# Linear attention and gated unit on one core: K's maxima and exponentials bank by bank, Q's maxima as rows, another opening and a new list

## The chip, the cores and the metric

One Trainium2 chip, one of its cores, one launch. The time is the device's microseconds for one execution. The kernel before took 234.67 us as the median of three runs (234.15 to 235.96). A profiled execution is a run by itself and has its own time, given below.

## The reference, cut to what matters

```python
def phi(x):                                        # x: 8 batches, 8 heads, 576 tokens, 64
    proj = np.einsum('bhsd,df->bhsf', x, w_phi)    # 128 features
    proj = proj - np.max(np.abs(proj), axis=-1, keepdims=True)
    return np.concatenate([np.exp(proj), np.exp(-proj)], axis=-1)
q_p, k_p = (phi(q), phi(k))
kv = np.einsum('bhsf,bhsd->bhfd', k_p, v);  z = np.sum(k_p, axis=2)
num = np.einsum('bhsf,bhfd->bhsd', q_p, kv)
den = np.einsum('bhsf,bhf->bhs', q_p, z)[..., None] + 1e-06
x = num / den                                      # heads side by side: 8 x 576 x 512
# gate_pre: a causal convolution of 5 taps along the tokens, per channel, of x
return (sigmoid(gate_pre) * (x @ w_val)) @ w_out
```

Note that the second half is exp(-proj) of the shifted projection: for the token t with maximum m it is exp(-p + m), so the shift has to reach both signs.

## The kernel before, in words

**Units.** A batch has 8 heads, taken as 4 pairs; a pair is a unit (numbers 0 to 31), with 512 of its 576 tokens. The 64 tokens left over in each of a batch's heads make one more unit (32 to 39, the tail units). After four units and a tail unit the batch's attention is complete, and its gated unit can run.

**A unit's steps**, with the names that the list uses: T transposes the unit's K and Q on the tensor engine (PE) into one bank of PSUM; C copies them out as bf16 (DVE or ACT). PK projects K (two banks, 4 x 2 x 128 columns of float32), MK takes the maxima of its absolute values over the features (DVE, line 441, one instruction over both banks), K0 and K1 take exp(p) and exp(-p) (ACT, line 475, one instruction each over both banks). E takes the exponentials of K's maxima (ACT, line 459) and V multiplies V's rows with them (POOL, line 505), so that K's shift is put into V. PA projects Q a first time with tokens on the partitions, only so that MQ (DVE, line 441) can take its maxima; PQ projects Q again with features on the partitions (line 541), SA subtracts the maxima in PSUM by 8 matmuls of a broadcast weight against a negative identity (line 564), and X0 and X1 take the two exponentials (ACT, line 466). KV (line 518) sums up K's features against V, KM copies the sum out, N (line 610) multiplies Q's features with it, XN divides (DVE, lines 628 and 630), and XP transposes the result by DMA or, late in the program, on PE (line 655). Per batch there are GF (the five taps as 80 matmuls, line 689), TH (tanh on ACT, line 705), VA and VB (x times w_val, line 710), GV (gate times value on DVE, line 726), OA and OB (times w_out, line 739), OE (ACT or DVE, lines 748 and 750) and the stores ST and SL; GT, VT, HT, GW, OT, OF and SU are the same for the 64 tokens left over (lines 779 to 824).

**What sets the order.** A string ORDER is a hand-made list of tokens. A token `PK.3@4,5:W` says: step PK of unit 3, PSUM banks 4 and 5, variant W; `:D`, `:A`, `:P` name DVE, ACT or POOL. Each engine works off its instructions in the order of the list, and semaphores hold them until their inputs are there. All eight banks of PSUM are dealt out by hand. Two engines that read the same bank are kept apart: a K exponential and the maxima of the same banks run one after the other. What stands ahead of the list (loads of the first unit, constants) was put in order by the scheduler. FL is a filler, a matmul of zeros.

**The opening.** The first unit's K comes in two halves on the queues of SP and ACT (line 169), Q follows in one piece on SP's queue (line 163), w_phi twice on ACT's queue (line 183) and is cast by `W.0:A` into W2 (line 223). All of w_val (1 MB) is loaded at the start (line 317) and cast by POOL in eleven pieces (CV). The other loads (LD) go through POOL's queue, with a cast. w_out is loaded by eleven DMAs on SP's queue (line 324) and cast whole on POOL (`CO.0:P`, the row `WOUT`).

## Time and profile before

| | |
|---|---|
| median of three runs | 234.67 us |
| the profiled execution | 232.76 us |
| its span (first to last instruction) | 231.0 us |
| PE busy | 206.4 us, 3758 matmuls |
| ACT busy | 185.8 us, 288 instructions |
| DVE busy | 178.7 us, 281 instructions |
| POOL busy | 134.2 us, 187 instructions |
| granted clock of PE | 1.00 in every stretch |

The span leaves out 1.8 us that lie around the program. An engine's busy time is the union of its instructions; where they follow one another without a wait, the next one starts before the one ahead has ended, so that a row's mean duration times its count is more than its busy time. A matmul's end is modelled. The views used are the table of busy time by stretches (`windows`), the groups of instructions by line and shape, the waits, the timeline, and the chain of waits, which is followed back from the last instruction.

### The profile page before, as it was taken

The page shows a single profiled execution, that of the slowest core. Times are in us where ns is not written, and L with a number is a line of the kernel's source. Part 1 is how long each engine was busy: PE and PEld are TensorE (multiplying, and loading weights), DVE is VectorE, ACT ScalarE, POOL GpSimd, SP SyncE. Part 2 cuts the span into 40 slices and gives each one's busy share as a digit, 9 for nine tenths or more (in the row PEclk, how much of TensorE's full clock was granted, in tenths as well). Part 3 has the DMA queues.
Part 4 walks back from the last instruction along what each step waited for, and adds up shares of the span by engine and source line. Part 5 has one row for each costly group of instructions (what it writes and reads, how often), then busy time and mean ns, then how long its engine had stood idle before and what let it go on. Part 6 is the DMA issues. An engine that isn't in the chain of part 4 may idle for free. (4 is left out here: it accounts for less than half of the span.)

```text
span 231.0 us, 8642 instructions
## 1 busy us (share of the span) xinstructions
PE 206.4 (89%) x3758; PEld 142.7 (62%) x3784; DVE 178.7 (77%) x281; ACT 185.8 (80%) x288; POOL 134.2 (58%) x187
## 2 busy tenths in 40 slices
PE   1567889899989589999998999899999999999996
PEld 0244677677658356568666866686668756675542
DVE  7298699989977669788886999699988897356341
ACT  2299999999879668988898989799898999652450
POOL 8479999995798199673316909720439248600000
DMA  6999999399999959999995198281682066103646
GB/s 130 263 186 161 173 145 144 37 194 199 129 179 220 217 63 160 146 187 136 128 181 192 27 139 164 70 116 26 154 168 71 4 93 184 45 7 91 176 144 184
DMA packets 41424, 31.36 MB, mean 136 GB/s; under 512 B 16933, under 2 KB 37413, under 8 KB 41386
## 3 DMA queue, kind: packets, MB, share of 16 engines
q0 software_dynamic: 20816, 14.90, 45.3%
q1 hardware_dynamic: 19946, 15.16, 32.6%
q10 hardware_dynamic: 624, 0.75, 1.1%
q8 instruction: 29, 0.48, 0.9%
q14 instruction: 9, 0.07, 0.1%
HBM read 32.58 MB, written 9.44 MB: 182 GB/s over the span
## 5 line engine op out<-in xcount | busy, mean ns | idle before, releaser
L505 POOL TENSOR_TENSOR VT<-vN,EA 128x1024 bf16<-128x1024 bf16 x32 | 61.1, 1910 | 22.7 <-issue 8.8
L475 ACT ACTIVATE KT<-PS 128x1024 bf16<-128x1024 f32 x64 | 63.9, 1041 | 5.1 <-PE PS L406 3.9
L466 ACT ACTIVATE QT<-PS 128x1024 bf16<-128x1024 f32 x64 | 62.1, 1043 | 6.0 <-PE PS L564 5.8
L441 DVE TENSOR_REDUCE MKA<-PS 128x8 f32<-128x1024 f32 (+1 forms) x40 | 44.3, 1112 | 5.5 <-PE PS L399 2.2
L441 DVE TENSOR_REDUCE MQA<-PS 128x8 bf16<-128x1024 f32 (+1 forms) x40 | 44.5, 1113 | 3.3 <-PE PS L406 2.1
L710 PE MATMUL PS<-XT,WVAL 128*128 128x512 bf16 x128 | 35.3, 380 | 0.2
L739 PE MATMUL PS<-WOUT,GV 128*128 128x512 bf16 x110 | 31.2, 380 | 2.5 <-POOL WOUT L225 1.8
L726 DVE SCALAR_TENSOR_TENSOR GV<-GATE,PS 128x512 bf16<-128x512 bf16 x32 | 21.3, 683 | 10.9 <-ACT GATE L705 6.1
L496 POOL TENSOR_TENSOR VTZ<-vN,EA 64x512 bf16<-64x512 bf16 x16 | 16.7, 1044 | 19.6 <-ACT EA L459 17.6
L564 PE MATMUL PS<-nident,MQA 128*128 128x128 bf16 x288 | 23.0, 220 | 2.8 <-issue 2.1
L225 DVE COPY T<-PS 128x1024 bf16<-128x1024 bf16 x29 | 19.6, 685 | 7.0 <-PE PS L366 6.7
L630 DVE TENSOR_TENSOR XN<-PS,RCPA 128x512 bf16<-128x512 f32 x32 | 22.1, 692 | 1.2 <-DVE RCPA L628 0.2
L564 PEld LDWEIGHTS <-MQA 128*128 128x128 bf16 x288 | 17.4, 98 | 8.4 <-issue 3.6
L518 PE MATMUL PS<-VT,KT 128*128 128x65 bf16 x512 | 21.9, 194 | 0.8 <-POOL VT L509 0.3
L610 PEld LDWEIGHTS <-QT 128*128 128x128 bf16 x512 | 19.3, 97 | 5.1 <-issue 0.5
L518 PEld LDWEIGHTS <-KT 128*128 128x128 bf16 x512 | 19.1, 98 | 4.4 <-issue 1.1
L610 PE MATMUL PS<-KVSA,QT 128*128 128x65 bf16 x512 | 21.0, 193 | 0.4 <-issue 0.2
L748 ACT ACTIVATE OS<-PS 128x512 f32<-128x512 f32 x24 | 13.8, 599 | 8.5 <-PE PS L739 6.3
L705 ACT ACTIVATE GATE<-PS 128x1024 bf16<-128x1024 f32 x16 | 16.0, 1039 | 5.2 <-PE PS L689 5.2
L406 PE MATMUL PS<-W,T 64*128 64x128 bf16 x392 | 18.7, 221 | 1.1 <-DVE MQA L441 0.4
L406 PEld LDWEIGHTS <-T 64*128 64x128 bf16 x392 | 13.0, 95 | 9.4 <-issue 5.7
L366 PE MATMUL PS<-ident_bf,kN 128*128 128x128 bf16 x128 | 12.8, 224 | 4.1 <-DVE kN L225 3.5
(93 smaller groups left out, 328.4 us busy)
## 6 DMA issues: line engine op xcount, KB each, us to landing
out_dram<-OS SPq DMA_DIRECT2D x28, 256.0 KB, 3.7
kN<-in_k_dram POOLq DMA_DIRECT2D x14, 320.0 KB, 7.4
vN<-in_v_dram POOLq DMA_DIRECT2D x14, 320.0 KB, 7.5
qN<-in_q_dram POOLq DMA_DIRECT2D x7, 576.0 KB, 9.0
OS<-in_moe_w_val_dram SPq DMA_DIRECT2D x1, 1024.0 KB, 10.4
out_dram<-OSt SPq DMA_DIRECT2D x8, 128.0 KB, 2.4
vN<-in_v_dram POOLq DMA_DIRECT2D x4, 160.0 KB, 7.4
OS<-in_moe_w_out_dram SPq DMA_DIRECT2D x8, 64.0 KB, 6.8
```

Of the source, the lines that this page charges most:

```text
L406: nc.tensor.matmul(PS[:, bank[par], c0 + blk * P:c0 + (blk + 1) * P], u.T[r, i, blk, :], W2[r, :], start=True, stop=True,)
L441: read(nc.vector.tensor_reduce(tokdst(dst[:, 0:n, :], wide, u.tail), tokview(bank, x, u, wide), AX.X, ALU.max, apply_absolute_value=True,) ...
L466: read(nc.scalar.activation(dst, banks(*bank)[:, :, 0:n * P].rearrange("p r (x t) -> p r x t", t=dst.shape[-1]), AF.Exp, scale=1.0 if ft = ...
L475: read(nc.scalar.activation(tokdst(u.KT[:, ft, :, :, :], u.PKwide, u.tail), tokview(u.PK, 0, u, u.PKwide), AF.Exp, scale=1.0 if ft == 0 el ...
L505: e.tensor_tensor(u.VT[:, :, :, 0:D], x.unsqueeze(1).to_broadcast([P, 2, n, D]), w.unsqueeze(3).to_broadcast([P, 2, n, D]), ALU.mult,)
L518: nc.tensor.matmul(PS[:, bank[0], c:c + E1], u.KT[:, ft, j // 2, j % 2, :], u.VT[:, ft, j, :], start=(ft == 0 and j == 0), stop=False, ski ...
L564: nc.tensor.matmul(PS[:, u.PQ[par], blk * P:(blk + 1) * P], MQA[:, i, blk, par:par + 1].to_broadcast([P, P]), nident[:, :], start=False, s ...
L610: nc.tensor.matmul(PS[:, bank[c // 2], x * E1:(x + 1) * E1], u.QT[:, ft, c, h2, :, :].rearrange("p j t -> p (j t)"), kv[:, ft, h2, :], sta ...
L630: read(nc.vector.tensor_tensor(u.XN[:, :, :, :], nv[:, :, :, 0:D], rc.unsqueeze(3).to_broadcast([P, 2, 4, D]), ALU.mult,), u.N)
L710: nc.tensor.matmul(PS[:, m.val[jt], :], WVAL[:, dt, jt * P:(jt + 1) * P], planes(xt(m.b), slice(0, P), dt, 4), start=(dt == 0), stop=(dt = ...
L726: read(nc.vector.scalar_tensor_tensor(out=m.GV[:, jt, :, :, :].rearrange("p n i t -> p (n i t)"), in0=m.GATE[jt // 2][:, jt % 2, :], scala ...
L739: nc.tensor.matmul(PS[:, bank, :], lhs(jt), WOUT[:, jt, :], start=(jt == 0), stop=(jt == 3))
```

## The change

**K bank by bank.** MK is replaced by MA and MB, one maximum per bank (line 503), and K0 and K1 by KA and KB, which take both exponentials of one bank (line 532). A bank is so released when its own pieces are done. Tail units keep the old steps.

**Q's maxima as rows.** For units 2 to 31 MQ writes its maxima into a row block MQX; a new step MT transposes it on PE (line 554, one matmul and one bank), MC copies it out as MQT (14 on ACT, 16 on DVE, 128x128), and SA's 8 matmuls take a broadcast column of the negative identity as weight and 64 of MQT's rows as input (line 661), where they took 128 rows.

**Opening.** Q's first load is in two halves, on the queues of SP and ACT behind K's. w_phi is one DMA on POOL's queue that reads it twice and casts it (line 195), so W is gone. T.0 is cut in two (T.0 for K, TX.0 for Q), and so is C.0 (C.0 on DVE, CX.0 on ACT). The constants of DVE stand in program order and all ahead of the first cast of Q. w_val's load stands later in the list (LW.0, after E.2).

**Early casts.** CV is four pieces, CO four pieces on DVE and POOL, and DIAGF's 16 copies are four (DF). w_out comes in six DMAs, and stands in the list before the first batch's gated unit, where it stood behind the second batch's gate steps (GT.1).

**List.** All tokens are dealt again over engines and banks: three V move from POOL to DVE, six OE from ACT to DVE, four T from DVE to ACT; 11 of 15 wide projections of K (PK:W, four matmuls of 256 columns) become narrow (eight of 128 with 64 rows).

On DVE at the start of the program (the instructions in order; XT, DIAGF, VTZ and MQX are constants, GV holds the loaded float32, T is the transposed unit) stood before:

```order
L213 MEMSET DIAGF 128x1280
L225 CAST kN<-GV 128x640
L198 CAST ident_123<-ident_bf 5x5
L255 TENSOR_SCALAR nident<-ident_bf 128x128
L225 CAST qN<-GV 128x576
L225 COPY T<-PS 128x1024 x2
L441 TENSOR_REDUCE MQA<-PS 128x2x4
L441 TENSOR_REDUCE MKA<-PS 128x2x4
```

and now:

```order
L224 MEMSET DIAGF 128x1280
L226 MEMSET VTZ_138 128x1040
L230 MEMSET MQX 128x256
L268 MEMSET VTZ_139 128x1040
L241 CAST qN<-GV 128x576
L241 COPY T<-PS 128x512
L503 TENSOR_REDUCE MKA<-PS 128x4 x2
L241 COPY T<-PS 128x1024
L472 TENSOR_REDUCE MQA<-PS 128x2x4 x2
```

K's cast has left DVE, the copy of the first transposes is half as long but still stands behind Q's cast, and the first maxima are two of one bank.

On ACT at the same place (W is w_phi in bf16, KT and QT the exponentials of K and Q) stood before:

```order
L190 ACTIVATE warm<-zero 128x1
L223 ACTIVATE W_129<-wtmp 128x128
L475 ACTIVATE KT<-PS 128x2x4x128 x4
L466 ACTIVATE QT<-PS 128x2x8x64
L223 ACTIVATE T<-PS 128x1024
L466 ACTIVATE QT<-PS 128x2x8x64
L475 ACTIVATE KTt<-PS 128x512
```

and now, with the waits:

```order
L202 ACTIVATE warm<-zero 128x1 [waits DVE_49]
L239 ACTIVATE kN<-GV 128x640 [waits DMAHW1_49,DMAHW0_49]
L239 ACTIVATE T<-PS 128x512 [waits PE_49]
L532 ACTIVATE KT<-PS 128x4x128 [waits DVE_49]
L532 ACTIVATE KT<-PS 128x4x128
L532 ACTIVATE KT<-PS 128x4x128 [waits DVE_49]
L532 ACTIVATE KT<-PS 128x4x128
L532 ACTIVATE KT<-PS 128x4x128 [waits PE_49]
L532 ACTIVATE KT<-PS 128x4x128 x3
L570 ACTIVATE QT<-PS 128x2x8x64 [waits PE_49]
```

Four exponentials of two banks have become eight of one, and the first pair of each bank waits for DVE's maximum of that bank.

At the end of the program ACT had (GATE is the last batch's tanh, GATEt that of the 64 tokens left over, OS the output):

```order
L799 ACTIVATE GATEt<-PS 128x256
L705 ACTIVATE GATE_4947<-PS 128x1024
L705 ACTIVATE GATE_4955<-PS 128x1024
L748 ACTIVATE OSt<-PS 128x512
L748 ACTIVATE OS<-PS 128x512 x2
L760 DMA out_dram<-OS 64x512 x4
```

and has now:

```order
L794 ACTIVATE GATE_5088<-PS 128x1024
L794 ACTIVATE GATE_5127<-PS 128x1024
L843 ACTIVATE OS<-PS 128x512
L894 ACTIVATE GATEt<-PS 128x256
L855 DMA out_dram<-OS 64x512
L843 ACTIVATE OS<-PS 128x512
L855 DMA out_dram<-OS 64x512 x2
L843 ACTIVATE OS<-PS 128x512
L855 DMA out_dram<-OS 64x512
L843 ACTIVATE OSt<-PS 128x512
```

The output of the 64 tokens left over (OSt) was ahead of the last batch's outputs and is now the last of all, behind ACT's four stores; its gate stands behind the last taps.

The diff, cut to its core:

```diff
 ORDER = """
-CK.0:D LD.0 ND.0:D LD.1 W.0:A FL.18@0 CQ.0:D LD.2 T.0@0 C.0:D FL.7@1 LD.3 FL.17@1 PK.0@0,1 K0.0 K1.0 T.1@2
...
+LD.1 CK.0:A LC.0 VZ.0:D CQ.0:D T.0@7 FL.16@6 C.0:D LD.0 TX.0@0 PK.0@6,2 T.1@1 CX.0:A PA.0@4,5 MA.0 MB.0 LD.3
...
+    main_dma((nc.sync, nc.scalar), "k", 0, 0, 1, first["k"])
+    for t in range(2):
+        (nc.sync, nc.scalar)[t].dma_start(
+            first["q"][t * 64:(t + 1) * 64, 0, :, :].rearrange("p j d -> p (j d)"),
+            q[0, t, :, :].rearrange("(p j) d -> p (j d)", j=J),
+        )
+    W2 = const.tile([P, F], BF16, name="W2")
+    nc.gpsimd.dma_start(W2[:, :], w_phi.unsqueeze(0).to_broadcast([2, D, F]))
...
+    MQX = const.tile([P, NG, P], BF16, name="MQX")
+    nc.vector.memset(MQX[:, :, :].rearrange("p g c -> p (g c)"), 0.0)
+    MQT = const.tile([P, NG, P], BF16, name="MQT")
...
+        w = moe_w_out.rearrange("(x r) o -> r x o", r=32)
+        for c, x, n, step in ((0, 0, 4, 5), (1, 1, 2, 3), (1, 11, 2, 3), (2, 2, 2, 5), (2, 8, 2, 5), (3, 3, 4, 3)):
...
+    def op_CO(jt, eng):
+        copy(eng, WOUT[:, jt, :], stage[1][:, jt, :])
...
+            c = i % G * 4
+            read(nc.vector.tensor_reduce(
+                MQX[:, i // G % NG, :].rearrange("p (r c) -> p r c", r=2)[:, :, c:c + 4],
+                tokview(u.PA, 0, u, None), AX.X, ALU.max, apply_absolute_value=True,
+            ), u.PA)
+
+    def half_view(t, x, wide):
+        return t[:, 2 * x:2 * x + 2] if wide else t[:, :, x:x + 1]
+
+    def half_ps(bank, x, t, wide):
+        n = t.shape[2]
+        b = t.shape[1]
+        return PS[:, bank[x], 0:b * n * F].rearrange("p (b r f) -> p b r f", b=b, f=F)
+
+    def halfmax(u, dst, bank, x, wide):
+        out = half_view(dst, x, wide)
+        read(nc.vector.tensor_reduce(
+            out, half_ps(bank, x, out, wide), AX.X, ALU.max, apply_absolute_value=True,
+        ), [bank[x]])
+
+    def op_MA(i, x=0):
+        u = units[i]
+        halfmax(u, MKA[:, i, :, :], u.PK, x, u.PKwide)
...
+    def op_KA(i, x=0):
+        u = units[i]
+        if not hasattr(u, "KT"):
+            u.KT = featk.tile([P, 2, 4, 2, F], BF16, name="KT")
+        for ft in range(2):
+            out = half_view(u.KT[:, ft, :, :, :], x, u.PKwide)
+            read(nc.scalar.activation(
+                out, half_ps(u.PK, x, out, u.PKwide), AF.Exp, scale=1.0 if ft == 0 else -1.0,
+            ), [u.PK[x]])
...
+    def op_MT(i, bank):
+        units[i].MT = PS[:, bank[0], 0:64].bitcast(BF16), bank
+        nc.tensor.transpose(units[i].MT[0], MQX[:, i // G % NG, :], ident_bf[:, :])
+
+    def op_MC(i, eng):
+        x, bank = units[i].MT
+        copy(eng, MQT[:, i // G % NG, :], x, bank)
...
+                else:
+                    r = slice(par * 64, par * 64 + 64)
+                    c = par * 64 + i % G * 4 + blk
+                    lhs, rhs = nident[r, c:c + 1].to_broadcast([64, P]), MQT[r, i // G % NG, :]
+                nc.tensor.matmul(cols, lhs, rhs, start=False, stop=True, skip_group_check=True)
```

More of the change, by code (lines that the diff above doesn't have):

```diff
@@ L268, in op_WB @@
             r = slice(x * 64, x * 64 + 64)
-            copy(eng, W2Z[r, x, :], wtmp[r, :])
+            copy(eng, W2Z[r, x, :], W2[r, :])
     def op_FL(i, bank):
@@ L305, in op_DG, with op_DF, blocks @@
         )
[L306 to L310 removed]
+    def op_DF(r, eng):
+        rows = slice(r * 32, r * 32 + 32)
+        copy(eng, blocks(rows, r), DIAG[rows, :, :, :].rearrange("p (x y) t c -> p x y t c", x=2))
+    def blocks(rows, r):
+        ap = DIAGF[rows, :, :, :].rearrange("p (x y) t c -> p x y t c", x=2)[:, :, :, :, 0:32]
+        steps = [list(x) for x in ap.ap]
+        steps[1][0] += 64 if r < 2 else -64
+        steps[2][0] += 32 if r % 2 == 0 else -32
+        return bass.AP(tensor=ap.tensor, offset=ap.offset + r * 32, ap=steps)
@@ L326, in op_CV @@
[L326 to L336 removed]
+            nc.sync.dma_start(stage[0][:, :, :], moe_w_val.rearrange("(a p) j -> p a j", p=P))
@@ new lines, in op_KB, with op_XA, op_XB @@
+    def op_KB(i):
+        op_KA(i, 1)
+    def op_XA(i, x=0):
+        u = units[i]
+        if not hasattr(u, "QT"):
+            u.QT = featq.tile([P, 2, 4, 2, 2, 64], BF16, name="QT")
+        for ft in range(2):
+            dst = u.QT[:, ft, :, :, x, :].rearrange("p c h t -> p (c h) t")
+            read(nc.scalar.activation(
+                dst, PS[:, u.PQ[x], :].rearrange("p (x t) -> p x t", t=64), AF.Exp, scale=1.0 if ft == 0 else -1.0,
+            ), [u.PQ[x]])
+    def op_XB(i):
+        op_XA(i, 1)
```

332 lines of the change are left out of this document (166 added, 166 removed).

## The prediction

> **What bounds the kernel now.** I read the page's busy times first, then the same by stretches, then the waits, and last the timeline at both ends.
>
> ```profile
> core 0: us, PE busy (x) PEld busy (x) DVE busy (x) ACT busy (x) POOL busy (x), PEclk, DMA share, GB/s
> 0.00:10.00 10.00, 2.61 (x11) 1.01 (x11) 5.38 (x12) 1.79 (x3) 6.75 (x17) 1.00 0.79 187
> 10.00:60.00 50.00, 43.47 (x833) 33.58 (x836) 43.19 (x62) 48.76 (x76) 43.34 (x73) 1.00 1.07 157
> 60.00:200.00 140.00, 131.93 (x2494) 91.96 (x2511) 116.98 (x183) 124.20 (x192) 81.67 (x96) 1.00 0.79 128
> 200.00:231.00 31.00, 28.39 (x425) 16.14 (x427) 13.15 (x26) 11.06 (x18) 2.43 (x4) 1.00 0.43 121
> ```
>
> There are four stages with four answers. Up to 10 us next to nothing runs: the first data is awaited. From 10 to 60 ACT is busy 48.76 of 50 us, so this stage lasts as long as ACT's list. From 60 to 200 PE is the busiest (131.93 of 140), with ACT (124.20) and DVE (116.98) close behind. From 200 on PE is alone. The clock is 1.00 throughout, so it explains nothing here.
>
> ```profile
> PE PS L739 <- POOL WOUT L225: 1.8, 1, 1.8
> POOL WOUT L225 <- DMA OS<-in_moe_w_out_dram: 5.4, 1, 5.4
> ACT KT L475 <- DVE MKA L441: 0.9, 2, 0.7
> ```
>
> Of the named waits few are long. PE stands 1.8 us for the cast of w_out, which had itself waited 5.4 us for its DMA; and the third row shows the readers of one pair of banks kept apart.
>
> **The opening.** The rows that set its end are these:
>
> ```profile
> 1.26 0.78 POOL L169 DMA_DIRECT2D kN<-in_k_dram  x1 [0.33 <-issue]
> 4.83 0.43 DVE L225 CAST kN<-GV 128x640 bf16<-128x640 f32 x1
> 7.91 0.31 ACT L223 ACTIVATE W<-wtmp 128x128 bf16<-128x128 f32 x1 [3.62 <-DMA wtmp<-in_w_phi_dram]
> 8.01 0.55 DVE L225 CAST qN<-GV 128x576 bf16<-128x576 f32 x1 [2.48 <-DMA GV<-in_q_dram]
> 10.01 0.61 PE L406 MATMUL PS<-W,T 64*128 64x128 bf16 x8
> 10.65 1.94 ACT L475 ACTIVATE KT<-PS 128x1024 bf16<-128x1024 f32 x2 [2.43 <-PE PS L406]
> ...
> GV<-in_q_dram SPq DMA_DIRECT2D x1, 288.0 KB, 6.4
> GV<-in_k_dram SPq DMA_DIRECT2D x1, 160.0 KB, 3.9
> kN<-in_k_dram POOLq DMA_DIRECT2D x2, 80.0 KB, 4.9
> qN<-in_q_dram POOLq DMA_DIRECT2D x1, 144.0 KB, 7.3
> OS<-in_moe_w_val_dram SPq DMA_DIRECT2D x1, 1024.0 KB, 10.4
> ```
>
> Q lands at 8.0, W is cast at 8.2, and the copy of the first transposes waits for both of the unit's halves; ACT's first exponential comes at 10.65. Now Q's halves are 144 KB each on two queues, and the 1024 KB of w_val no longer run beside them. A half of K (160 KB) took 3.9 us, the whole Q 6.4; issued at about 1.5 us, Q then lands between 5.4 and 8.0, and I take 6.0, nearer the row of its own size. Q's cast still stands ahead of C.0 on DVE: 6.0 + 0.55 + some 0.4 for the half copy makes 7.0 for PK.0. w_phi must be there too: one DMA of POOL's queue issued at about 1.6; its nearest row is kN's 80 KB with 4.9 us, so 6.5; by qN's 144 KB with 7.3 it would be 8.9. Then a first maximum of one bank (0.68 in a row below), and the first exponential at about 8.3: **-2.3 us**. Bounds: 0 (PK.0 again after 8.9, with its first copy late as well) and -3.0 (all landing at 5.4). CK's and CX's work on ACT fits ahead of that and costs nothing; it would cost 0.6 each if K landed late.
>
> **Splitting K's instructions.** These rows carry the price:
>
> ```profile
> L475 ACT ACTIVATE KT<-PS 128x1024 bf16<-128x1024 f32 x64 | 63.9, 1041 | 5.1 <-PE PS L406 3.9 <-DVE MKA L441 0.9
> L475 ACT ACTIVATE KTt<-PS 128x512 bf16<-128x512 f32 x16 | 9.2, 627 | 0.9 <-PE PS L406 0.9
> L441 DVE TENSOR_REDUCE MKA<-PS 128x8 f32<-128x1024 f32 x32 | 38.9, 1220 | 5.5 <-PE PS L399 2.2 <-PE PS L406 2.2 <-ACT KT L475 0.7
> L441 DVE TENSOR_REDUCE MKA<-PS 128x4 f32<-128x512 f32 x8 | 5.4, 680 | 0.0
> ...
> 21.77 3.80 ACT L466 ACTIVATE QT<-PS 128x1024 bf16<-128x1024 f32 x4
> 18.32 1.09 ACT L466 ACTIVATE QTt<-PS 128x512 bf16<-128x512 f32 x2
> ```
>
> By single durations 64 exponentials of 1024 become 128 of 512: 128 x 0.627 - 64 x 1.041 = +13.6 us on ACT. But instructions that follow one another overlap: four of 1024 take 3.80, so one costs (3.80 - 1.04)/3 = 0.92; two of 512 take 1.09, so one costs 1.09 - 0.60 = 0.49. That makes 128 x 0.49 - 64 x 0.92 = +3.8. DVE's maxima go the same way: 64 x 0.60 - 32 x 1.14 = +1.9 back to back, 64 x 0.680 - 32 x 1.220 = +4.5 by durations. I take the back-to-back figures, since both pieces' inputs come from one run of matmuls.
>
> [...]
>
> What the split buys is the banks: a pair was held for 1.22 + 1.94 = 3.2 us after its matmuls; now one bank is free after 0.68 + 1.09 = 1.8 and the other after about 2.9, since DVE reads one while ACT reads the other.
>
> **The rest of ACT's and DVE's list.** ACT: 14 copies of 128x128 (about 0.16 each back to back, worked out from 0.38 at 256 and 0.60 at 512 elements) +2.2; four T +3.7 (0.92 each); six OE, one OSt, two Tt and three KM fewer, -5.2; in all with the split about +4.8, of which some 1.0 lies in ACT's idle opening. DVE: split +1.9; 16 copies +2.1; three V, not seen on DVE: between 1.2 (twice XN's 0.69 less its fixed part) and 1.91 (POOL's own time), I take 1.25, +3.8; seven output copies at 0.60 +4.2; three KM, two casts of w_out, the two DF, two Tt and HL +3.5; five T fewer -3.0. About **+12.5** in all.
>
> ```profile
> L630 DVE TENSOR_TENSOR XN<-PS,RCPA 128x512 bf16<-128x512 f32 x32 | 22.1, 692 | 1.2 <-DVE RCPA L628 0.2
> L505 POOL TENSOR_TENSOR VT<-vN,EA 128x1024 bf16<-128x1024 bf16 x32 | 61.1, 1910 | 22.7 <-issue 8.8 <-ACT EA L459 8.0 <-DMA vN<-in_v_dram 5.6
> L748 ACT ACTIVATE OS<-PS 128x512 f32<-128x512 f32 x24 | 13.8, 599 | 8.5 <-PE PS L739 6.3 <-POOL VT L509 2.0
> L223 ACT ACTIVATE XT<-PS 128x256 bf16<-128x256 bf16 x3 | 1.2, 384 | 1.6 <-PE PS L645 1.6
> ```
>
> In the stage to 60 us ACT sets the pace, so its list up to there counts in full: about a quarter of +3.8, **+1.0** (bounds 0 and +4, the latter if DVE, at 43.19 of 50 before, becomes the bound).
>
> **PE.** SA's matmuls keep their count but use 64 rows; the chain shows such pairs back to back:
>
> ```profile
> 190.74 0.33 PE PS L406 x8
> 189.86 0.45 PE PS L564 x8
> 184.10 0.45 PE PS L366 x8
> ...
> L399 PE MATMUL PS<-W2Z,T 128*128 128x256 bf16 x60 | 9.0, 273 | 0.5 <-DVE T L225 0.3 <-DVE MQA L441 0.2
> ```
>
> 30 units x (0.45 - 0.33) = -3.6; 30 transposes x 0.056 = +1.7; 11 units' wide PK to narrow, between -0.1 (0.45 less 0.33, the wide one being 4 x twice 0.056) and -0.27 (4 x 9.0/60 less 0.33) each, -1.5. Sum about -3.5. Two thirds lie in the stage from 60 to 200, where PE leads: **-2.5** (bounds 0, if ACT or DVE is what is waited for, and -3.5). w_out stands far ahead of its first use now: **-1.8**, the wait above; bound 0 if the wait moves to another DMA. Banks released earlier: 0 to -4, I take **-1.5** of the 8 us that PE stands idle in that stage. Against it DVE's list: it had 23 us idle there and gets some 8 more work; at 125 of 140 busy it will be late for PE now and then: **+1.5** (bounds 0 and +6). The new chain of a Q unit, MQ, MT, MC, SA, adds a matmul and a copy (about 0.6 us) ahead of SA; PE has other units' work there, and queued behind a late MC on PE are the exponentials' inputs, so this is part of the +1.5.
>
> **The end.** Before:
>
> ```profile
> 214.84 0.84 PEld L779 LDWEIGHTS <-DIAGF 128*128 128x128 bf16 x20
> 217.76 1.35 PE L689 MATMUL PS<-XT,DIAG 32*32 32x512 bf16 x80
> 219.04 2.33 PE L710 MATMUL PS<-XT,WVAL 128*128 128x512 bf16 x10
> 222.07 3.62 PE L739 MATMUL PS<-WOUT,GV 128*128 128x512 bf16 x16
> 224.44 2.68 ACTq L760 DMA_DIRECT2D out_dram<-OS  x4
> 225.73 0.69 DVE L750 TENSOR_SCALAR OS<-PS 128x512 f32<-128x512 f32 x1 [0.17 <-PE PS L739]
> ```
>
> After the last taps (219.1) 30 matmuls of 512 columns followed, and the span ended 11.9 us later. Now GT and VT of the last batch (20 and 16 small matmuls, about 1.1) come behind the taps too, and on ACT the last output stands behind four stores of 2.68/4 = 0.67 and two output copies: I work out the end at about 13.5 after the taps, +1.6. Two units' Q exponentials also move behind the last but one taps: PE's list between the two gains about 0.7, of which 0.4 counts. **+2.0** (bounds +0.5 and +3.5).
>
> **Sum.** -2.3 + 1.0 - 2.5 - 1.8 - 1.5 + 1.5 + 2.0 = -3.6. The profiled execution's span becomes 227.4 and its time 232.76 - 3.6 = 229.2; the median of the runs lay 1.9 above that execution, so 234.67 - 3.6 = **231.1 us**. The runs before spread from 234.15 to 235.96, so that about 1% (2.3 us) is what can be told from no change.
>
> **Rivals.**
>
> *The halves do not run back to back (slower).* KA waits for DVE's maximum of its bank. Decides from: more than half of the K halves starting after an idle gap. Then ACT pays durations, +13.6 for +3.8, so 9.8 more, and DVE 2.6 more; ACT's list sets the time to 60 (+2.5) and overtakes PE after it (124 + 3 + 6 + 2 of 140, with PE's and the banks' gains of 4.0 gone): 231.1 + 2.5 + 4.0 + 1 = 238.6. For it: the waits in the listed order. Against: both banks' matmuls end within 0.2 us. [...] Chance 0.12.
>
> *DVE becomes the bound (no change).* +12.5 us on an engine that was busy 43.19 of 50 in the second stage: +3 there for +1.0, PE's -2.5 not seen, but the other terms kept: 231.1 + 2.0 + 2.5 = 235.6, or 234 if half of it. Chance 0.24.
>
> *w_phi is late.* Its DMA is 128 pieces from a source that is read twice; as slow as qN's 144 KB it lands at 8.9, the opening's gain shrinks to -0.4 and the time is 233.0. [...] Chance 0.16.
>
> *The banks were the real limit.* PE, ACT and DVE are all below 95% from 60 to 200, and DMA waits explain little. If the release gives its whole 4 and PE its 3.5, and the second stage nothing lost: 231.1 - 2.5 - 1.0 - 1.0 - 1.5 = 225.1. Chance 0.14. The forecast has 0.34.
>
> **How the numbers follow.** Under 232.3 (1% faster) lie the forecast mostly, the last rival wholly, and a little of the third and second: 0.57. Over 237.0 lie the first rival and the worst of the second: 0.15. The rest is 0.28. The range is 225.5 to 237.0: it leaves out about half of the last rival and the first.
>
> **What would show it.** Right: the first K exponential on ACT near 8.3 us; no wait for WOUT; KT pieces at a union of about 0.5 each; DVE near 191 and ACT near 190 busy; last taps' end to span end near 13.5. Wrong: KT halves behind gaps for MKA; a PK.0 that waits for w_phi's DMA; DVE at 95% and more after 60 us; a GF stage no earlier than before.

## The result, and the profile after

The kernel after took 245.42 us (median of 4 runs, 243.7 to 246.77), the kernel before on the same chip 234.41 (4 runs): ratio 1.0452, 95% interval 1.0363 to 1.0541. It is slower, and the forecast of 231.1 and its range were wrong. In a control further down, the same pair gave 242.98 and 234.28, ratio 1.0327 (1.0256 to 1.0397). Executions of the kernel before spread by 2 to 4% on each chip that had eleven or more of them, from 230.4 to 240.1 over all chips; medians below hold all runs, ratios leave out the slower ones, so the two can stand a little apart.

The profiled execution of after took 244.54 us with a span of 242.8. First the windows of the prediction:

```profile
core 0: us, PE busy (x) PEld busy (x) DVE busy (x) ACT busy (x) POOL busy (x), PEclk, DMA share, GB/s
0.00:10.00 10.00, 3.00 (x25) 1.91 (x25) 6.45 (x17) 3.21 (x5) 7.82 (x18) 1.00 0.90 146
10.00:60.00 50.00, 39.73 (x729) 30.61 (x730) 43.80 (x78) 43.69 (x83) 34.69 (x45) 0.88 0.98 169
60.00:200.00 140.00, 125.15 (x2461) 85.14 (x2480) 117.33 (x213) 121.56 (x231) 72.73 (x89) 0.98 0.71 117
200.00:242.80 42.80, 39.50 (x618) 23.41 (x623) 25.09 (x47) 24.72 (x43) 8.19 (x7) 1.00 0.48 118
```

From 10 to 60 no engine is at its limit any more. ACT, which had 48.76 of 50, is down to 43.69, and DVE is level with it; POOL lost 8.7 us of work. The clock, 1.00 before, is 0.88.

Windows of equal length hide where the time went, since the same work no longer stands in them. So I cut both spans at the same work: the first gate (the first tanh of batch 0), the gate of batch 2, and the end of the last taps. Before:

```profile
0.00:48.50 48.50, 35.17 (x602) 25.60 (x606) 37.90 (x56) 39.19 (x62) 42.36 (x80) 1.00 0.96 156
48.50:98.10 49.60, 44.01 (x869) 31.20 (x874) 40.93 (x63) 42.87 (x66) 37.60 (x46) 1.00 1.15 166
98.10:219.10 121.00, 117.67 (x2253) 81.72 (x2267) 96.00 (x156) 100.03 (x159) 54.23 (x62) 1.00 0.61 112
219.10:231.00 11.90, 9.56 (x45) 4.17 (x44) 3.87 (x6) 3.73 (x5) 0.00 (x0) 1.00 0.55 167
```

and after:

```profile
0.00:52.30 52.30, 37.19 (x649) 27.96 (x652) 44.96 (x84) 41.41 (x80) 38.10 (x56) 0.90 0.92 161
52.30:108.60 56.30, 45.69 (x880) 31.33 (x885) 43.66 (x78) 44.55 (x84) 33.20 (x43) 0.94 0.89 134
108.60:229.00 120.40, 113.58 (x2222) 76.48 (x2243) 100.36 (x185) 102.64 (x191) 52.13 (x60) 1.00 0.60 110
229.00:242.80 13.80, 10.92 (x79) 5.29 (x81) 3.68 (x6) 4.59 (x7) 0.00 (x0) 1.00 0.51 153
```

The second column is the length of each stretch: +3.8, +6.7, -0.6 and +1.9 us, together the 11.8 of the span. The third, between the gate of batch 2 and the last taps, is even a little faster. The loss lies ahead of 108 us and at the end. In the first stretch DVE has 7.1 us more to do (44.96 for 37.90) and ACT 2.2. In the second the work of PE, DVE and ACT is only 1.7 to 2.7 us more, but the stretch is 6.7 longer: waits.

Each of these is one execution, and one execution's gates move. The first tanh of batches 0, 1 and 2 in the traces of this and the kernels further down, in us:

| kernel | batch 0 | batch 1 | batch 2 |
|---|---|---|---|
| before | 48.5 | 71.6 | 98.1 |
| b5 (before; other loads from 43 us on) | 50.5 | 77.4 | 100.3 |
| b3 (before; DVE loaded) | 53.8 | 78.8 | 101.6 |
| b4 (before; DVE loaded twice) | 55.9 | 82.4 | 106.4 |
| after | 52.3 | 79.8 | 108.6 |
| c0 (after, unaltered) | 51.7 | 78.4 | 106.3 |
| e4 | 52.5 | 77.3 | 105.4 |
| e5 | 50.9 | 76.1 | 105.6 |
| e6 | 51.7 | 78.5 | 103.4 |
| e8 | 50.4 | 72.7 | 99.6 |
| e12 | 52.8 | 75.3 | 101.1 |

b5 has the list of before up to 43 us and was already 2.0 us behind it at 21 us. So of the +3.8 to the first gate, up to 2 can be the luck of the execution of before; the loss between the gates of batches 0 and 2 is clear of that (49.6 and 49.8 us in before and b5, 56.3 and 54.6 in after and c0).

The waits that answer to the three rows before, and two new ones (in all, times, longest, us):

```profile
PE PS L778 <- DVE XT L241: 4.5, 1, 4.5
...
DVE XT L241 <- issue: 4.4, 1, 4.4
...
ACT KT L532 <- DVE MKA L503: 2.9, 6, 0.7
...
PE PS L622 <- DVE XN L719: 2.1, 1, 2.1
DVE WOUT L241 <- DMA OS<-in_moe_w_out_dram: 2.0, 1, 2.0
```

PE no longer waits for w_out, but DVE does: a piece of the cast, CO.2, stands in DVE's queue ahead of the division XN of unit 5, and PE waits behind both. In the timeline:

```profile
54.70 0.43 DVE L241 CAST WOUT<-OS 128x512 bf16<-128x512 f32 x1 [1.98 <-DMA OS<-in_moe_w_out_dram]
55.28 0.69 DVE L719 TENSOR_TENSOR XN<-PS,RCPA 128x512 bf16<-128x512 f32 x1
56.03 0.69 PE L622 MATMUL PS<-VT,KT 128*128 128x65 bf16 x16 [2.06 <-DVE XN L719]
...
105.67 0.43 DVE L241 COPY XT<-XT 128x1008 bf16<-128x1008 bf16 x1 [4.39 <-issue]
...
106.15 1.47 PE L778 MATMUL PS<-XT,DIAG 32*32 32x512 bf16 x38 [4.47 <-DVE XT L241]
```

The second pair is the dearer. HL.2 copies the halo of batch 2 out of XT and so needs its four transposes by DMA; the list issues them in one block at 93.46 to 99.1, the last landed at 105.5, 7.6 us after its issue, and the taps GF.2 stand right behind. From 102.2 to 105.6 PE and DVE did nothing and ACT 1.2 us. In before the four were issued from 76.2 to 88.4, and the taps waited for none of them.

The opening:

```profile
1.43 1.00 POOL L195 DMA_DIRECT2D W<-in_w_phi_dram  x1
...
7.18 0.46 DVE L241 CAST qN<-GV 128x576 bf16<-128x576 f32 x1 [1.12 <-DMA GV<-in_q_dram]
7.55 0.42 DVE L241 COPY T<-PS 128x512 bf16<-128x512 bf16 x1
7.58 0.63 POOL L241 COPY W2Z<-W 64x128 bf16<-64x128 bf16 x2 [1.39 <-DMA W<-in_w_phi_dram]
...
8.24 0.61 PE L437 MATMUL PS<-W,T 64*128 64x128 bf16 x8
...
8.88 1.29 DVE L503 TENSOR_REDUCE MKA<-PS 128x4 f32<-128x512 f32 x2 [0.91 <-PE PS L437]
...
9.61 2.61 ACT L532 ACTIVATE KT<-PS 128x512 bf16<-128x512 f32 x5 [0.67 <-DVE MKA L503]
```

The first exponential is at 9.61 (I had 8.3), because Q's second half landed at 7.1 where I took 6.0, and K's copy stands behind Q's cast. The 10.65 of before was a late one: in the four other traces with the old opening (b1, b3, b4, b5 below) Q's cast began between 6.30 and 7.85 and the first exponential at 8.86 to 10.40; in the thirteen with the new opening (all but e1, which joins the halves again) the cast began at 6.69 to 7.82 and the exponential at 9.12 to 10.24. A gain of the new opening can't be told from this spread.

The groups:

```profile
L532 ACT ACTIVATE KT<-PS 128x512 bf16<-128x512 f32 x128 | 68.4, 618 | 4.1 <-DVE MKA L503 2.9 <-PE PS L437 1.1
...
L503 DVE TENSOR_REDUCE MKA<-PS 128x4 f32<-128x512 f32 x64 | 42.4, 683 | 4.5 <-PE PS L437 4.3
...
L609 DVE TENSOR_TENSOR VT<-vN,EA 128x1024 bf16<-128x1024 bf16 x3 | 4.4, 1453 | 0.0
```

128 pieces of K's exponential in 68.4 us are 0.53 each, +4.5 for the 64 pairs (forecast +3.8); the maxima are +3.5 (forecast +1.9). The new copies MC take 4.1 us of ACT and 3.5 of DVE (forecast 2.2 and 2.1).

### The profile page after: what moved, and what is told of

The parts are those of the page before. It is cut to its first block, busy times and chain, and to the rows that moved or that the text cites. A ratio compares the mean times of both kernels' runs of the same rounds, so it can differ in the third digit from the quotient of the medians.

```text
span 242.8 us, 8891 instructions
## 1 busy us (share of the span) xinstructions
PE 207.4 (85%) x3823; PEld 141.1 (58%) x3854; DVE 192.7 (79%) x352; ACT 193.2 (80%) x360; POOL 123.4 (51%) x158
## 4 chain that ended last, share of the span: by engine, by line
PE 51%; DVE 20%; DMA 9%; ACT 8%; issue 7%; POOL 1%; SPq 1%; ACTq 1%; DVEq 0%; POOLq 0%
PE PS L834 9%; PE PS L805 8%; PE PS L437 5%; PE PS L622 5%; DVE MKA L503 5%; PE PS L699 4%; DMA XT<-XN 4%; ACT QT L570 4%; PE PS L778 4%; DVE XN L719 4%; DVE MQX L488 3%; PE PS L387 3%; DMA OS<-in_moe_w_out_dram 3%; PE PS L661 3%; PE PS L645 2%
## 5 line engine op out<-in xcount | busy, mean ns | idle before, releaser
L532 ACT ACTIVATE KT<-PS 128x512 bf16<-128x512 f32 x128 | 68.4, 618 | 4.1 <-DVE MKA L503 2.9
L609 POOL TENSOR_TENSOR VT<-vN,EA 128x1024 bf16<-128x1024 bf16 x29 | 55.3, 1908 | 29.9 <-issue 24.0
L503 DVE TENSOR_REDUCE MKA<-PS 128x4 f32<-128x512 f32 x64 | 42.4, 683 | 4.5 <-PE PS L437 4.3
L488 DVE TENSOR_REDUCE MQX<-PS 128x8 bf16<-128x1024 f32 x30 | 36.3, 1218 | 1.8 <-PE PS L437 1.6
L437 PE MATMUL PS<-W,T 64*128 64x128 bf16 x480 | 25.9, 229 | 4.0 <-issue 0.9
L437 PEld LDWEIGHTS <-T 64*128 64x128 bf16 x480 | 16.7, 98 | 15.3 <-issue 11.8
L241 DVE COPY T<-PS 128x1024 bf16<-128x1024 bf16 (+1 forms) x25 | 16.8, 674 | 1.9 <-PE PS L387 1.8
L843 ACT ACTIVATE OS<-PS 128x512 f32<-128x512 f32 x18 | 11.1, 616 | 7.7 <-issue 4.9
L778 PE MATMUL PS<-XT,DIAG 32*32 32x512 bf16 x640 | 12.2, 408 | 5.0 <-DVE XT L241 4.5
L387 PEld LDWEIGHTS <-kN 128*128 128x128 bf16 x128 | 9.2, 103 | 10.3 <-ACT kN L239 5.5
```

The source lines that it names most:

```text
L387: nc.tensor.transpose(u.Tps[:, x, blk, :], a, ident_bf[:, :])
L437: nc.tensor.matmul(PS[:, bank[par], c0 + blk * P:c0 + (blk + 1) * P], u.T[r, i, blk, :], W2[r, :], start=True, stop=True,)
L488: read(nc.vector.tensor_reduce(MQX[:, i // G % NG, :].rearrange("p (r c) -> p r c", r=2)[:, :, c:c + 4], tokview(u.PA, 0, u, None), AX.X, ...
L503: read(nc.vector.tensor_reduce(out, half_ps(bank, x, out, wide), AX.X, ALU.max, apply_absolute_value=True,), [bank[x]])
L532: read(nc.scalar.activation(out, half_ps(u.PK, x, out, u.PKwide), AF.Exp, scale=1.0 if ft == 0 else -1.0,), [u.PK[x]])
L609: e.tensor_tensor(u.VT[:, :, :, 0:D], x.unsqueeze(1).to_broadcast([P, 2, n, D]), w.unsqueeze(3).to_broadcast([P, 2, n, D]), ALU.mult,)
```

## Experiments: the new instructions by themselves

Three theories stood after this. "Clock": PE starves, its clock falls, and that is the loss. "Instructions": the halves and rows cost too much. "Late data" or "the list": the waits above. The kernels are named by what they change; b is made from the kernel before, e from the kernel after.

**b1: the split alone, in the kernel before.**

```diff
-MK.i  K0.i  K1.i
+MA.i MB.i  KA.i  KB.i      (units 0 to 31, places kept)
```

> The kernel before, its list unchanged but for K: each maximum over a pair of banks is two in a row over one bank each, each pair of exponentials becomes four of one bank each, the first bank's two at the place of the first, the other's two at the place of the second. Theory 'clock': the split itself is worth little either way where PE stays fed: 232 to 238 us, clock 1.00. Theory 'instructions': ACT and DVE pay some +4 and +2 us and more for gaps between the pieces: 238 to 244, with the clock at 1.00.

236.82 us against 234.69, ratio 1.0048 (0.9968 to 1.0128): no difference that can be told. "Instructions" falls for the split, and in that list no gain from the banks can be seen either.

**e1: the split undone, in the kernel after.**

```diff
-MA.i MB.i  KA.i  KB.i
+MK.i  K0.i  K1.i           (units 0 to 31)
```

> The changed kernel's list, but K's maximum and exponentials again over the pair of banks (one instruction where the change has two; where a bank is filled again between the two places, both stand at the first). Theory 'clock': the changed kernel loses its time because PE is starved in places, the granted clock then falls to half (17 us of half clock in the profiled run, worth up to 8.5 us) and the whole waits by what it is late; the width of K's instructions has little to do with it: 241 to 248 us, mean clock still under 0.98. Theory 'instructions': the halves cost ACT and DVE more than they give back; without them ACT is about 188 busy and DVE about 189, and the time falls to 237 to 241.

291.63 us (286.09 to 292.94) against 234.69, far outside both. Its waits, PE's and ACT's:

```profile
ACT KT L572 <- DVE MKA L465: 11.7, 11, 1.7
...
PE PS L430 <- ACT KT L572: 7.4, 6, 2.0
...
PE PS L798 <- ACT KT L572: 5.0, 4, 3.1
```

The new list fills a bank again right behind its own half; with pairs every such place waits for the other bank too, and there both banks' instructions had to stand at the first one's place. So the release bank by bank is real, and the list is built on it. But what a release is worth depends on the list: nothing that can be told in the old one, some 46 us, with those moves, in the new.

**e2: Q's maxima as columns again, in the kernel after.**

```diff
-MT.i@b MC.i:e              (units 2 to 31)
...
-elif i < 2:
+else:                      (MQ writes MQA, SA reads it with 128 rows)
```

> The changed kernel's list without the rows for Q's maxima: no transpose of MQX, no copy to MQT, SA reads the column of maxima as before with 128 rows. Theory 'clock': one link of the chain MQ, MT, MC, SA is gone, two of PE's waits in the first 40 us with it, but the long stalls at 54 and 102 us stay: 240 to 245, clock 0.95 to 0.98. Theory 'instructions': 30 copies fewer (ACT about -2.2 us, DVE about -2.1 us): 241 to 244 with the stalls and the clock as they were. A result above 246 would say that the rows help and only the rest of the change costs.

245.5 against 234.69, ratio 1.054 (1.0402 to 1.0678): above both ranges, and not to be told from after. The rows neither cause the loss nor hold it back by an amount that can be seen.

**b2: the opening alone, in the kernel before.**

```diff
-T.0@0 C.0:D ... PK.0@0,1 K0.0 K1.0
+T.0@0 C.0:D CQ.0:D ... PK.0@0,1 TX.0@2 CX.0:A K0.0 K1.0
```

> The kernel before with the changed kernel's opening alone: Q's first half units on two queues, w_phi by one converting DMA of POOL's queue, the first transposes and their copy in two halves (Q's copied by ACT), Q's cast behind the copy of K's half, and one filler fewer. If the opening is worth what the prediction's term says, -2.3 us in full: 231 to 233.5. If only as much as the first exponential moved in the changed kernel (-1.0 us): 233 to 235. If the stage behind it swallows the gain (ACT was already busy 98% to the first gate, but its inputs then come no earlier): 234 to 236.5.

234.28 against 234.59, ratio 1.0061 (0.9999 to 1.0123): no gain. It is no clean test of the term. In its profiled execution w_phi's DMA, issued at 1.28, took 9.2 us to land, and PE waited for it:

```profile
10.49 0.61 PE L419 MATMUL PS<-W,T 64*128 64x128 bf16 x8 [3.64 <-DMA W<-in_w_phi_dram]
```

ACT's copy CX.0, which I had put ahead of the exponentials, so came at 11.68 and they began at 12.17. This is the rival "w_phi is late" of the prediction. Here the 1 MB of w_val is loaded beside it, as in before; in the thirteen traces above, where w_val comes later, the same DMA landed 5.6 to 6.6 us after its issue. That w_val is the reason wasn't tried by itself.

**b5: w_out loaded early, in the kernel before.**

```diff
-... HL.1:P V.8 LW.1 LD.14
+... XP.3 LW.1 SA.7:F
```

> The kernel before with the eight loads of w_out issued behind the transpose XP.3 (about 45 us) instead of behind HL.1 (62 to 73 us); the cast stays where it is. If the term of the prediction is right (PE's wait of 1.8 us goes): 232 to 233.5 where the kernel before has about 234.4. If the loads collide with those of the next batch, or the wait moves to another datum: 234 to 237.

234.41 against 233.8. PE's wait for the cast is gone from the trace, and five of six executions took 233.3 to 236.6 (the sixth 229.44). A gain of 1.8 us is not to be seen in the median.

## Experiments: the clock

The page of after shows the granted clock in 40 slices:

```profile
PEclk9996797997999999979999999999999999999999
```

In its record the clock changes only after whole multiples of 3.41 us: four stretches at half clock last 6.83, 3.41, 3.41 and 3.41 us, those at full clock between them 10.24, 17.07 and 44.37. The window of 3.41 us ahead of each fall, and below them what followed the first:

```profile
16.88:20.30 3.42, 1.75 (x26) 1.05 (x23) 3.39 (x5) 3.42 (x11) 0.86 (x2) 1.00 1.32 196
33.95:37.36 3.41, 1.40 (x33) 1.16 (x32) 3.31 (x8) 2.74 (x6) 1.75 (x3) 1.00 0.80 141
54.43:57.84 3.41, 1.81 (x45) 1.43 (x46) 3.04 (x6) 2.11 (x4) 2.27 (x4) 1.00 1.29 178
102.21:105.62 3.41, 0.00 (x0) 0.00 (x0) 0.00 (x0) 1.19 (x2) 3.41 (x5) 1.00 1.27 217
...
20.30:27.12 6.82, 6.04 (x69) 4.27 (x67) 5.47 (x10) 5.18 (x11) 5.88 (x8) 0.50 1.35 202
```

PE (the second number) was busy 1.75, 1.40, 1.81 and 0.00 us of 3.41, and the clock went to 0.50. The falls at 20.30, 37.36, 57.84 and 105.63 lie 17.07, 20.48 and 47.79 us apart, 5, 6 and 14 times 3.41. By my estimate the 17.1 us at half clock could be worth up to 8.5. (A matmul's end is modelled, so the busy times here are too.)

**e3: PE fed.**

```diff
+FL.30@2 FL.31@2 FL.32@2 MT.3@7
...
+FL.41@4 ... FL.46@4 KV.4@0
...
+FL.52@6 ... FL.63@6 GF.2@2,3,6,7     (42 fillers at ten places)
```

> The changed kernel with 42 more matmuls of zeros by zeros (512 columns, about 0.21 us each back to back) on free banks, put ahead of ten places where PE stood idle for 0.4 to 4.5 us; nothing else differs. Theory 'clock': PE is kept busy, the half-clock stretches after these places vanish or become fewer (mean clock 0.98 to 1.00), and the time falls by what they cost: 236 to 241. Theory 'stalls alone' (the waits themselves cost, not the clock) and theory 'instructions': the fillers only fill idle time, 244 to 248, whatever the clock is.

242.89 against 234.69, ratio 1.0451 (1.036 to 1.0543): as slow as after, at a clock of 0.98 to 1.00. The window behind the first fillers, at full clock now:

```profile
20.30:27.12 6.82, 5.35 (x87) 3.35 (x85) 6.39 (x13) 6.78 (x14) 5.40 (x7) 1.00 1.36 203
```

PE did 87 matmuls where it had done 69, and the first KV came at 29.92 (29.74 in after): behind DVE and ACT, a faster PE bought nothing. The time lies between the ranges of both theories; most of the loss is there at nearly full clock, unless the fillers cost something themselves.

**e10: the same with the waits repaired** (28 fillers at nine places in the kernel e9 below; the expectation says 26).

> The kernel of e9_end with 26 matmuls of zeros ahead of nine places where the changed kernel's PE stood idle. If the half clock costs time once the waits are gone: clock 0.99 to 1.00 and 1 to 3 us less than e9_end. If the clock falls only where PE waits anyhow: within 1 us of e9_end, whatever the clock.

242.29, ratio 1.0368 (1.0298 to 1.0439), against 235.3 and 1.0083 for e9. Neither outcome came: with the fillers it takes 7 us more, at a clock of 0.96 to 0.99. So fillers are not free, e3 may hold a loss of its own beside whatever it gained, and the price of the half clock stays open. e8 below bounds it: 234 us at a clock of 0.97 to 0.985, with 6.8 us at half clock in its trace for the 17.1 of after. The 10 us less could be worth 5 at most; what they were worth wasn't separated.

## Experiments: DVE's list and late data

**e4: late data off DVE.**

```diff
-CO.2:D  CO.3:D  HL.2:D
+CO.1:P CO.2:P CO.3:P  HL.2:P
-LD.18 ... LD.14
+LD.14 ... GF.2@2,3,6,7 LD.18
```

> The changed kernel with its late-data waits taken off DVE's list: the casts CO.2 and CO.3 of w_out go to POOL behind CO.1, the copy HL.2 goes to POOL, and the load of v for batch 3 changes place with that of k for batch 5, which moves behind GF.2, so that no load runs beside the four transposes by DMA ahead of HL.2. Theory 'late data' (DVE's 2.0 us for w_out at 54.7 and PE's 4.5 us for XT at 101.7 are lost once each and never regained): 237 to 240.5 us, first gate of batch 2 about 5 us earlier than 108.6. Theory 'DVE is short in the first stage' (the gate of batch 0 is already 3.8 us late and the late data only use up slack that would be lost anyway): 241.5 to 245.

241.1 against 234.59, ratio 1.0424 (1.0372 to 1.0476). PE's wait ahead of GF.2 only changed its name:

```profile
101.84 1.02 POOL L236 COPY XT<-XT 128x1008 bf16<-128x1008 bf16 x1 [8.83 <-DMA XT<-XN]
102.91 1.51 PE L773 MATMUL PS<-XT,DIAG 32*32 32x512 bf16 x48 [3.78 <-POOL XT L236]
```

With the copy on another engine and the load away, most of it stays: the four transposes are issued too late. The time lies between the two ranges.

**e5: DVE relieved up to the first gate.**

```diff
-V.0:D  DF.2:D  DF.1:D  HL.0:D
+V.0:P  DF.0:P DF.2:P DF.1:P  HL.0:P
```

> The changed kernel with four instructions of the first 52 us back from DVE to POOL: the V of unit 0, the block copies DF.1 and DF.2 (behind DF.0) and HL.0; some 3.7 us of DVE. Theory 'DVE is short in the first stage' (DVE is busy 45.3 of 52.3 us up to the first gate, ACT 41.4; before 37.9 and 39.4 of 48.5): the first gate comes at 49.5 to 51 instead of 52.3, and the time is 240 to 243. Theory 'late data': first gate within 1 us of 52.3 and 243.5 to 247, since POOL's V of units 0 and 2 come later.

239.85 against 234.59, ratio 1.0268 (1.0142 to 1.0394), with the first gate at 50.9 as the first theory had it: better than e4, but by itself not clear of the control's 1.0327.

**b3 and b4: DVE loaded, in the kernel before.** The converse, with seven and with fourteen memsets of 0.59 us that nobody reads.

```diff
+nc.vector.memset(dummy[:, i % 2, :], 0.0)
-MK.1 ... MK.2 ... MK.32 ... MK.3 ...
+MK.1 XD.0 ... MK.2 XD.1 ... MK.32 XD.2 ... MK.3 XD.3 ...
```

> The kernel before with seven memsets of 640 floats that nobody reads (about 0.6 to 1.1 us each) put on DVE between 15 and 38 us, behind MK.1, MK.2, MK.32, MK.3, XN.1, MK.4 and XN.0: some 4 to 7 us more for DVE up to the first gate, as much as the change adds there, and nothing else. Theory 'DVE is short in the first stage': the first gate of batch 0 moves from 48.5 to 50.5 to 54 and the time becomes 237 to 241. Theory 'late data' or 'the list': DVE had 9 us idle there and absorbs them, 234 to 236.5.

> The kernel before with fourteen memsets that nobody reads on DVE between 15 and 38 us instead of the seven of the earlier run: 14 x 0.59 = 8.3 us more for DVE up to the first gate, close to the 7.4 that the change adds there. Theory 'DVE is short in the first stage': 8.3 us less what DVE had idle there costs 4 to 9 us, 239 to 244. Theory 'late data' or 'the list' alone: 234 to 237.5.

b3: 236.14 against 234.59, ratio 1.0243 (1.0175 to 1.031). b4: 239.42 against 234.28, ratio 1.0209 (1.0141 to 1.0278). The trace of b4, up to its first gate:

```profile
0.00:55.90 55.90, 40.40 (x602) 29.77 (x605) 45.15 (x70) 39.91 (x62) 44.37 (x83) 0.94 0.85 143
```

and its group of memsets:

```profile
L272 DVE MEMSET dummy<- 128x640 f32 x14 | 8.3, 592 | 1.2
```

DVE has the 45 us that it has in after, and the first gate comes at 55.9 (b3: 53.8) for 48.5 and 50.5 in the two traces without the load. Both kernels are slower, though DVE had 10 us idle in that stretch. I read it so: ACT, busy 48.76 of the 50 us from 10 to 60, is fed by DVE, and by what DVE is late, ACT is late. In b4 ACT waits 2.6 us for DVE's maxima ahead of E, for which before has no such row. Once the work is added, the clock falls too (0.94). The ratios don't grow with the load as the medians do (+1.6 and +5.1), so the size is open, between 0.4 us (b3's median) and 1.4 us (its ratio) for each us of DVE; b3's gate is in the range of the first theory, its time in that of the other.

**c0 and e6: a control, and the transposes earlier.**

```diff
-XN.9 ... XN.8 ... XN.10 ... XP.10 ... XP.9 ... XN.11 XP.8 XP.11
+XN.9 XP.9 ... XN.8 XP.8 ... XN.10 XP.10 ... XN.11 XP.11
```

> The changed kernel unaltered, as a control beside the three others on the same chip: 243 to 247 us by every theory, clock 0.95 to 0.97.

> The changed kernel with three transposes by DMA of batch 2 (XP.8, XP.9, XP.10) issued right behind the division that feeds each, instead of all four together ahead of HL.2; nothing else moves. Theory 'late data': the fourth then has SP and the DMA engines to itself and lands some 3 us sooner, PE's wait ahead of GF.2 shrinks from 4.5 us to 1 to 2 and the time to 241 to 243. Theory 'DVE is short in the first stage' alone: the wait shrinks, but DVE and ACT were the ones behind, so 244 to 246.

c0: 242.98 against 234.28, ratio 1.0327 (1.0256 to 1.0397). e6 on the same chip: 240.58, ratio 1.0181 (1.0096 to 1.0267). Three tokens moved, and nearly half of the loss is gone (the intervals overlap by a hair). In e6:

```profile
101.98 1.35 PE L772 MATMUL PS<-XT,DIAG 32*32 32x512 bf16 x80 [1.61 <-DVE XT L235]
```

The wait is 1.6 us, for 3.6 in the control's trace and 4.5 in that of after.

**e7 and e8: the repairs together.** e7 has e4, e5 and e6; e8 leaves HL.2 and the two loads where the change had put them.

```diff
-V.0:D  DF.2:D  DF.1:D  HL.0:D  CO.2:D  CO.3:D
+V.0:P  DF.0:P DF.2:P DF.1:P  HL.0:P  CO.1:P CO.2:P CO.3:P
-XN.9 ... XN.8 ... XN.10 ... XP.10 ... XP.9 ... XN.11 XP.8 XP.11
+XN.9 XP.9 ... XN.8 XP.8 ... XN.10 XP.10 ... XN.11 XP.11
```

> The changed kernel with all three repairs: four instructions of the first stage back from DVE to POOL, the casts of w_out and the copy HL.2 on POOL and the two loads changed round, and the transposes of batch 2 issued early. Theory 'DVE is short in the first stage, and the waits for late data add to it': both gains add up, 234 to 237, and what is left against the kernel before is the end (+1.9 us) and the batches behind. If they share one slack: 238 to 241. If the half clock set the time by itself: 240 or more with the clock still under 0.98.

> The changed kernel with V of unit 0, DF.1, DF.2, HL.0 and the casts CO.2, CO.3 on POOL and the transposes XP.8 to XP.10 issued early; HL.2 stays on DVE and the loads stay where they are. Theory 'DVE is short in the first stage, and late data add to it': batch 3 is no longer late as it was with HL.2 and v's load moved, so 233 to 237. Theory 'one slack shared': 238 to 241, as with all repairs.

e7: 238.95, ratio 1.0114 (1.0053 to 1.0175). Its batch 3 took 33.1 us from gate to gate (26.6 in after): three V on POOL ran from 98.2 to 104.1, hardly sooner than in after (99.1 to 104.9), though the gate of batch 2 came 10 us earlier. e8: 233.96 against 233.8, ratio 1.0022 (0.9979 to 1.0064). Each was timed beside the kernel before on its own chip, and after itself not on that of e8. Six instructions from DVE to POOL and three transposes moved, and in e8 the loss is gone:

```profile
0.00:50.40 50.40, 36.65 (x650) 27.35 (x651) 41.81 (x79) 40.90 (x79) 40.54 (x61) 0.93 0.95 167
50.40:99.60 49.20, 43.71 (x889) 29.59 (x887) 43.72 (x75) 44.04 (x85) 35.28 (x44) 1.00 1.00 148
99.60:220.30 120.70, 115.17 (x2244) 76.39 (x2242) 101.43 (x187) 102.48 (x191) 52.85 (x62) 1.00 0.61 112
220.30:234.00 13.70, 11.12 (x81) 5.23 (x79) 3.68 (x6) 4.52 (x7) 0.00 (x0) 1.00 0.52 154
```

Against after the first stretch is 1.9 shorter with DVE at 41.81 for 44.96, the second 7.1, the others as they were. Between the gates of batches 0 and 2 the control takes 54.6 us, e5 54.8, e4 52.9, e6 51.7 and e8 49.2 (in executions of 241.66, 241.38, 240.07, 236.13 and 235.80 us): the transposes give the larger part, and no one repair gives it all. (How it divides over batches 1 and 2 can't be read: the gate of batch 1 comes 23.1 us behind the first in before and 26.9 in b5, and at batch 2 the two are level again.) PE's wait ahead of GF.2 is still 3.4 us in e8.

**e9: the end.** The last batch's tail gate ahead of its taps, as before, on e8.

```diff
-HL.7:D VA.28@0 GF.7@6,7,1,2 ... GT.7@6,7 ... HT.7 ... VT.7 GW.7
+GT.7@2,3 HT.7 VA.29@4 OE.25:D HL.7:D VT.7 ... GW.7 GF.7@6,7,0,1 VA.28@2
```

> The kernel of e8_three with the last batch's GT.7, HT.7, VT.7 and GW.7 ahead of its taps GF.7, as the kernel before had them; banks renumbered there. If the end costs what the prediction's term says (+2.0; in the trace 13.8 us behind the last taps for 11.9): the span behind the last taps falls to about 12 and the time by 1 to 2 us against e8_three. If GW.7 on DVE now delays the taps: no gain, within 0.5 us.

235.3, ratio 1.0083 (1.003 to 1.0136), and 14.4 us behind the last taps for 13.7: no gain. What makes the end longer is not the place of those steps. In the traces of after and e9 alike the last output is OSt, on ACT behind a store; no run moves it.

**e11 and e12: the same two mechanisms once more**, on e8.

```diff
-LD.18 ... LD.14
+LD.14 LD.18                 (e11)
-MT.i@b MC.i:e               (e12, units 2 to 7, on e11)
```

> The kernel of e8_three with the load of v for batch 3 (LD.14) issued some 10 us earlier, ahead of the load of k for batch 5, so that it doesn't run beside the last transpose ahead of HL.2. Theory 'late data': PE's 3.4 us ahead of GF.2 shrink to 1 to 2 and the time to 231.5 to 233. If that wait is set by the distance from XN.11 to GF.2 in the list and not by the load: 233.5 to 235.

> The kernel of e11_v_early with Q's maxima as columns for units 2 to 7 (as the change does for units 0 and 1): five copies MC of 0.2 us fewer on DVE and one of 0.3 on ACT up to the first gate, six transposes fewer on PE, SA there with 128 rows. Theory 'DVE is short in the first stage': 0.5 to 1.5 us less than e11_v_early, 230 to 232.5. If DVE is no longer what is waited for there: within 0.5 us of e11_v_early.

235.21, ratio 1.0136 (1.0065 to 1.0207), and 234.61, ratio 1.0126 (1.0063 to 1.0189), against 232.78. e11 is above both its ranges; e12 is within 0.5 us of it by the ratios, so 1 us less on DVE buys nothing there. In e11's trace PE's wait ahead of GF.2 is down to 1.6 us from 3.4 in e8, and the time is no shorter; what is waited for instead stays open. e7, e9, e11 and e12, which hold the repairs of e8 or nearly those and more, stand at 0.8 to 1.4% over the kernel before. None of these kernels beats it.

## Why the prediction was wrong, point by point

**The opening, -2.3: failed.** It came to -1.0 against the one trace that I had, and to nothing against the five of the old opening (8.86 to 10.65, after 9.61). I took one execution's landing of Q at 8.0 as the opening's, and it moves between 6.3 and 8.0 by itself; the halves landed no earlier (7.1, taken 6.0). The rival of w_phi at 8.9 did not come in after (landed at 7.4), where the wait for Q hid what was late of it; it came in b2 (10.5).

**The split:** its price was near for the exponentials (0.53 us each for 0.49) and low for the maxima (+3.5 for +1.9) and the copies MC (7.6 us for 4.3). My terms for ACT add up to +4.5, not the +4.8 that I wrote, and ACT's work grew by 7.4 (193.2 us for 185.8), DVE's by 14.0 (192.7). The rival of halves that do not run back to back didn't come: ACT waited 2.9 us for the maxima. In the list of before the split costs nothing that can be told (b1).

**The stage to 60 us, +1.0: this step failed.** I counted a quarter of ACT's extra and said "bounds 0 and +4, the latter if DVE, at 43.19 of 50 before, becomes the bound". It was +3.8 to the first gate in these two traces, 1.2 by those of b5 and c0. I had summed DVE's list over the whole program (+12.5, measured +14) and spread it; 7.1 of it stand ahead of the first gate, where ACT had next to no idle time and takes its input from DVE. It is the place that decides, and it could have been counted in the order of DVE's instructions. b3 and b4 show it by their gates (53.8 and 55.9). The way back is weaker: with those instructions off DVE the gate comes at 50.4 to 51.2 in six traces (e5, e7 to e11) for 51.7 to 52.5 in six without (after, c0, e2, e3, e4, e6), but e12, with less on DVE still, had it at 52.8.

**DVE late for PE, +1.5, and no term for late data: the larger failure.** I weighed DVE's idle time in the mean (23 us of 140) and took w_out's wait as gone, "bound 0 if the wait moves to another DMA". A wait in a list that was dealt again doesn't go, it moves: to CO.2 on DVE (2.0 us, with PE behind it) and to HL.2 (4.4 us, with PE, DVE and ACT behind it). Between the gates of batches 0 and 2, 6.7 us were lost. That the transposes stand too close to the taps is shown by e6 on the control's chip (wait 1.6 us for 3.6, time 1.0181 for 1.0327); e4, with the copy on POOL and the load away, kept 3.8 us of the wait. The rest is DVE's: e8, with six instructions off its list as well, takes 49.2 us there, where e6 takes 51.7.

**PE -2.5, w_out -1.8, banks -1.5: failed too.** PE's and the banks' came to -0.6 between 98 and 219 us, though PE did have 4.1 us less to do there (113.58 for 117.67, clock 1.00 in both): it stood idle instead, 6.8 us for 3.3. w_out's lies ahead of 98 us, where nothing was gained; b5 has the wait gone and no gain, and b1 the banks and no gain. An idle time taken from an engine that waits again at the next step is no gain.

**The end, +2.0:** +1.9. Its size is right, by luck in part: e9 shows that the place of GT.7 and VT.7, which I had counted in it, is not the cause. Of the output behind ACT's stores, the other half of my sum, no run decides.

**The rival "DVE becomes the bound"** named the mechanism of the first stage and its place; its price (235.6) lacked the waits behind. The clock, of which I wrote that it explains nothing, did not stay at 1.00. It fell behind windows in which PE was busy 0.00 to 1.81 us of 3.41, and e8 reaches 234 us with part of that fall; as the cause of the whole loss it is ruled out, as a part of it not.

## What to carry to other kernels

Where a list is dealt again, don't sum an engine's extra work over the program: count it stretch by stretch, ahead of each point where another engine waits for it, and price an engine that feeds a saturated one as part of that one's list. For each load or transpose by DMA, measure the distance in the new order from its issue to the first instruction that needs it, and look at what stands in the queue behind that instruction. Three transposes issued when their input was ready, and six instructions moved from DVE to POOL, won back all that the change had lost in e8, and most of it in its neighbours. And before a step is priced from one trace, look at how far other executions move it: the opening's gain was forecast from a landing that moved by 1.7 us by itself.
